# A passage from attention to a spectral layer: late output products grouped by half, one tile turned in the next PSUM pool, statistics taken later

## The chip, the core and the metric

The kernel runs on one core of one Trainium2 chip. The metric is the device time of one execution in microseconds (us), lower is better. Times of one kernel scatter: three runs of the kernel before gave 1471.8, 1475.76 and 1479.76 us, and the execution that was profiled took 1471.74 us.

## The reference

Four layers follow each other on `x` of 2048 rows by 576 columns, with a residual each: attention, spectral, attention, spectral.

```python
def _A_ref(x, wqkv, wo):              # H = 32 heads of 18, window W = 256
    q, k, v = (x @ wqkv) split into heads
    p = softmax(mask(q k^T * 18 ** -0.5))
    return (p v) @ wo
def _B_ref(x, w_r, w_i):
    X = rfft2(x) * (w_r + 1j * w_i)
    return irfft2(X, s=(S, D))
x = x + _A_ref(_layernorm(x), A_wqkv, A_wo)
x = x + _B_ref(_layernorm(x), B_w_r, B_w_i)
x = x + _A_ref(_layernorm(x), A_wqkv, A_wo)
x = x + _B_ref(_layernorm(x), B_w_r, B_w_i)
```

## The kernel before, in words

All orders are written out by hand: each engine runs its instructions in the order of the code, and semaphores that the framework adds from the tiles that are written and read make one engine wait for another. `layer_a` is an attention layer, `layer_b` the spectral layer that it calls at its end (`spectral`, line 1005). Both run twice, so that every passage from attention to the spectral layer occurs twice in the trace, near 477 to 500 us and near 1213 to 1237 us.

The passage is the output projection `o @ wo` plus residual, for 16 tiles of 128 rows. The class `Out` (line 442) holds it:

- `load` fetches a tile's attention output and its residual rows `x`; `tail` (GpSimd) and `turn` (TensorE transposes, then a copy and a subtraction) make the split stationary operands; `turn_last` and `split_last` do the same for the last 128 columns, which the last head group delivers at the very end. In the profile all stationary operands, weights and constants of this stage lie in one buffer `oroom`, everything in full precision (attention output, `x`, statistics) in `ofree`.
- A tile's projection is 28 products of 128x288: 14 pairs of a stationary and a moving operand, each for two halves of 288 columns. `early` (line 519) issues the 11 pairs that don't need the last columns, `late` (line 532) the other three pairs, then two adds on VectorE (line 538), one per half, of `x` and the half in PSUM, and the store. `steps` (line 513) is the loop over pairs and, inside, over the two halves.
- `unit` (line 555) does a whole tile: it takes one PSUM tile `ops`, 128 x 2 x 512, one half in each of two banks, calls `early` and `late`.
- `sums` and `stats` make the layer norm's statistics of the tile's new `x` (lines 545 and 546 on VectorE, a square root on ScalarE at line 547, two small VectorE operations at lines 551 and 552). `f0` (line 166) normalises and folds the row on ScalarE and GpSimd, and, for tile 0 only, with a subtraction on VectorE (line 173).

Tiles 0 to 2 are projected in the attention layer's PSUM pool, each half in a bank of its own tile (`ops0_0`, `ops0_1`, `ops1_S`, `ops1_E`, `ops2_E`, `ops2_pj`; lines 975 to 1004). The spectral layer then opens its own pool with the tags `mm` (three tiles of two banks), `tp` and `tq` (one bank each), and projects tiles 3 to 15 with `unit`, 13 a layer. Tiles 3 and 4 are interleaved with `norm` (that is `sums` and `f0`) of the first tiles (lines 241 to 255); from tile 5 on a loop over `t` (line 256) does, in this order: `unit(t + 4)`, `f1(t)` (transposes `tp`, `tq`), `sums`, `f3(t - 1)` (products `pz`), `f0(t + 4)`, `f2(t)` (products `pf`), and `ahead(t + 6)`, which loads, and turns the projection's operands of the tile two units ahead.

Where two banks of the old pool are taken over by a tile of the new one, that tile's first write waits until the old pool's readers are done.

Of the kernel before, what the change touches and what calls it, by code (L numbers as in the profile page):

```python
# [8 lines left out]
F32 = mybir.dt.float32  # L9
# [93 lines left out]
def layer_b(tc, src, dst, dcs, gc, ident, rh, rl, out, ic_d, fc_d, ga_d, m2_d, w_d, dram):  # L103

    nc = tc.nc
    V, A, T, P = nc.vector, nc.scalar, nc.tensor, nc.gpsimd
# [3 lines left out]
    with tc.tile_pool(name="bc", bufs=1) as cp, tc.tile_pool(name="bw", bufs=2) as wp, \  # L110
# [55 lines left out]
        def f0(n2, h):  # L166
            x, r, n = out.stats(n2)
            xn = wp.tile([128, D], F32, tag="ta", name=f"xn{n2}", bufs=3)
            A.activation(xn, x, AF.Identity, bias=n, scale=r)  # L169
            eo = h["eo"] = eos[n2 % 4]  # L170
            P.tensor_add(eo[:, 0, 1:288], xn[:, 1:288], xn[:, 575:288:-1])  # L171
            A.copy(eo[:, 0, 0:289:288], xn[:, 0:289:288])
            (P if n2 else V).tensor_sub(eo[:, 1, 0:287], xn[:, 1:288], xn[:, 575:288:-1])

            tl = h["tl"] = wp.tile([128, 2, 3, 33], F32, tag="td", name=f"tl{n2}", bufs=4)
            e = eo[:, :, 256:289]
            P.tensor_copy(tl[:, :, 0].bitcast(F32R), e)
            P.tensor_copy(tl[:, :, 2].bitcast(F32R), e)
            P.tensor_sub(tl[:, :, 1].bitcast(F32R), e, tl[:, :, 0])

        def turn(n2, x, tl):
            t4 = pp.tile([128, 512], F32, tag="tp", name=f"tp{n2}", bufs=1).rearrange("p (c a t) -> p c a t", c=2, a=2)
            tq = pp.tile([128, 512], F32, tag="tq", name=f"tq{n2}", bufs=1)[0:99, 0:256].rearrange("p (c t) -> p c t", c=2)
            for c in range(2):
                for a in range(2):
                    T.transpose(t4[:, c, a], x[:, c, 128 * a:128 * a + 128], ident)
            for c in range(2):
                T.transpose(tq[:, c], tl[:, c].rearrange("p a w -> p (a w)"), ident)
            et = wp.tile([128, 2, 4, 128], F32R, tag="tc", name=f"et{n2}", bufs=3)
            ett = wp.tile([99, 2, 128], F32R, tag="te", name=f"ett{n2}", bufs=3)  # L190
            A.copy(et[:, :, 0:2], t4)
            A.copy(ett, tq)
            V.tensor_sub(et[:, :, 2:4], t4, et[:, :, 0:2].bitcast(F32))
            return et, ett

        def rows(ps, ets, m):
            et, ett = ets
            for c in range(2):
                o = ps[:, c, 0:NF]
                seq = [(0, 0), (0, 2), (1, 1), (1, 3), (2, 0), (3, 1)]  # L200
                for q, (si, mi) in enumerate(seq):
                    T.matmul(o, et[:, c, si], m(5 * c + mi), start=q == 0, stop=False)  # L202
                T.matmul(o, ett[:, c], m(5 * c + 4)[0:99], start=False, stop=True)

        def f1(n2, h):
            eo, tl = h["eo"], h["tl"]
            h["et"] = turn(n2, eo, tl)

        def f2(n2, h):
            ps = pp.tile([128, 2, 512], F32, tag="mm", name=f"pf{n2}", bufs=3)  # L210
            rows(ps, h["et"], lambda k: dcs[k // 2][:, k % 2])
            h["yh"] = yh = wp.tile([128, 2, NF], F32R, tag="yh", name=f"yh{n2}", bufs=3)
            h["yl"] = yl = wp.tile([128, 2, NF], F32R, tag="yl", name=f"yl{n2}", bufs=3)
            A.copy(yh, ps[:, :, 0:NF])
            V.tensor_sub(yl, ps[:, :, 0:NF], yh.bitcast(F32))
# [21 lines left out]
        def norm(u):  # L237
            out.sums(u)
            f0(u, hs[u])

        f0(0, hs[0])
        out.load(5)
        norm(1)
        out.load(6)
        out.tail(5)
        out.unit(3, pp)
        norm(2)
        out.load(7)
        out.tail(6)
        f1(0, hs[0])  # L250
        out.unit(4, pp)
        f2(0, hs[0])
        out.ahead(5, pp)
        norm(3)
        out.tail(7)
        for t in range(1, NT - 4):
            u = t + 4
# [184 lines left out]
class Out:  # L442
# [67 lines left out]
        self.nc.scalar.copy(oL[:, 0:128], tp)  # L510
        self.nc.vector.tensor_sub(oL[:, 128:256], tp, oL[:, 0:128].bitcast(F32))

    def steps(self, u, ks, first, last):
        for i, (x, p, wk) in enumerate(ks):
            for n in range(2):
                self.nc.tensor.matmul(self.ps[u][n][:, 0:288], x, self.w[p][:, wk * D + n * 288:wk * D + n * 288 + 288],  # L516
                                      start=first and i == 0, stop=last and i == len(ks) - 1)

# [13 lines left out]
    def late(self, u):  # L532
        oL = self.oL[u % 3]
        h, l = oL[:, 0:128], oL[:, 128:256]
        self.steps(u, [(h, "h", 3), (l, "h", 3), (h, "l", 3)], False, True)
        x = self.x[u % 5]
        for n in range(2):
            self.nc.vector.tensor_add(x[:, n * 288:n * 288 + 288], x[:, n * 288:n * 288 + 288], self.ps[u][n][:, 0:288])
        self.nc.sync.dma_start(self.dstv[:, u], x)

# [29 lines left out]
def layer_a(tc, src, dst, wqk_d, wv_d, wo_d, dc_d, gc_d, dram, copy, wvs, wos, second, spectral):  # L570
    nc = tc.nc
    V, A, T, P = nc.vector, nc.scalar, nc.tensor, nc.gpsimd
# [7 lines left out]
    with ExitStack() as ctx:  # L580
# [129 lines left out]
        with ExitStack() as c2:  # L710
            wp = c2.enter_context(tc.tile_pool(name="a2", bufs=2))
            pp = c2.enter_context(tc.tile_pool(name="a2p", bufs=2, space=PSUM))
# [7 lines left out]
            for j in range(2):  # L720
                q = wp.tile([128, 2, S], F32R, name=f"qs{j}", bufs=1)
                k = wp.tile([128, 2, S], F32R, name=f"ks{j}", bufs=1)
# [171 lines left out]
            pj = [f for i in range(2, 9) for c in range(4) for f in proj(i, c, "E" if i == 2 and c % 2 else "pj", True)]  # L894
# [9 lines left out]
            out = Out(nc, ident, eps, bp, ov, o7v, srcv, dstv, wos, dc_d, gc_d)  # L904

            for t in range(-LEAD, NX + 2):
# [3 lines left out]
                n, c = divmod(t + 17, NT)  # L910
# [56 lines left out]
                if t - OB - 5 in (0, 1, 2):  # L967
                    u = t - OB - 5
# [8 lines left out]
            for k in range(4):  # L977
                tp = pp.tile([128, 512], F32, tag="E" if k in (1, 2) else "pj", name=f"tpz{k}", bufs=2)[0:32]
# [6 lines left out]
                             rc.to_broadcast([32, 4, 4, 18]))  # L985
            out.early(0, None, slice(4, 11))
            out.early(1, [pp.tile([128, 512], F32, tag=k, name=f"ops1_{k}", bufs=b) for k, b in (("S", 3), ("E", 2))])
            tp = pp.tile([128, 512], F32, tag="pj", name="tpl", bufs=2)
            for f in (out.turn_last, out.split_last):
                for u in range(3):  # L990
                    f(u, tp[:, 128 * u:128 * u + 128])
            out.early(2, [pp.tile([128, 512], F32, tag=k, name=f"ops2_{k}", bufs=2) for k in ("E", "pj")])
            out.turn(3, U, A)
            out.tail(4)
            for u in range(3):
                out.late(u)
                if u == 0:
                    out.turn_last(3, tp[:, 384:512])
                    out.split_last(3, tp[:, 384:512])
                    out.sums(u)  # L1000
                if u == 1:
                    out.turn_last(4, tp[:, 0:128])
                    out.split_last(4, tp[:, 0:128])
            out.turn(4, pp.tile([128, 512], F32, tag="E", name="tpa4", bufs=2), A)
        spectral(dst, out.dcs, out.gc, ident, out.rh, out.rl, out)
        ctx2.close()

# [1 line left out]
def prompt_kernel(tc, x, wqk, wv, wo, w, dc, ic, fc, gc, ga, m2, out):  # L1009
    with tc.tile_pool(name="dram", bufs=1, space=bass.MemoryType.DRAM) as dram, tc.manual_schedule():  # L1010
        t = [dram.tile([S, D], F32, name=f"x{i}") for i in range(3)]
        cr = {k: dram.tile(list(v.shape), F32R, name=k + "r") for k, v in (("dc", dc), ("ic", ic), ("gc", gc), ("ga", ga))}
        wvs, wos = [dram.tile([2, 128, 5 * D], F32R, name=k) for k in ("wvs", "wos")]
        for i, (s, a, d) in enumerate(((x, t[0], t[1]), (t[1], t[2], out))):
            with tc.tile_pool(name=f"dram{i}", bufs=1, space=bass.MemoryType.DRAM) as dr:
                layer_a(tc, s, a, wqk, wv, wo, cr["dc"], cr["gc"], dr, [(cr[k], v) for k, v in (("dc", dc), ("gc", gc), ("ic", ic), ("ga", ga))] if i == 0 else None, wvs, wos, i > 0,
                        lambda *args: layer_b(tc, args[0], d, *args[1:], cr["ic"], fc, cr["ga"], m2, w, dr))
# [18 lines left out]
```

## Time and profile before

| | us |
|---|---|
| three runs | 1471.8, 1475.76, 1479.76 (median 1475.76) |
| the profiled execution | 1471.74, of which the profile's span is 1470.0 |
| TensorE matmul busy | 1382.7 (94%) |
| VectorE, ScalarE, GpSimd busy | 950.0, 810.1, 714.0 |
| chain that ended last | PE 75%, DMA 9%, DVE 5%, ACT 4%, POOL 3% |

PE is TensorE's matmul, PEld its weight load, DVE VectorE, ACT ScalarE, POOL GpSimd, SP the engine that issues most DMAs. In a row of the timeline stand the start, the time until the end, the engine, the line, the operation, out<-in by the program's names (numbers left out), the shape, how many were merged into the row, and in brackets the idle time of the engine ahead of it with what ended it. A row with x and three numbers divided by strokes gives shortest, median and longest of a group in ns. The mean granted TensorE clock was 0.98 over the span.

### The profile page before, as it was taken

The numbers are of one execution on the slowest core, as the hardware profiler recorded it, in microseconds if no ns is written. First come the engines' busy times: TensorE is split into PE (matmuls) and PEld (weight loads), VectorE is DVE, ScalarE is ACT, GpSimd is POOL, SyncE is SP. The second block draws the span as 40 slices with busy tenths as digits, with TensorE's granted clock in tenths as the row PEclk, the third lists the DMA queues.
The fourth block names the chain that finished last, engine by engine and source line by source line (L and its number), as shares of the span: only waits on it lengthen the run. The fifth ranks groups of instructions, "written<-read, shape, count | busy, mean of one in ns | idle before, by whom it ended". The sixth has DMA issues, their size and how long they took to land.

```text
span 1470.0 us, 35320 instructions
## 1 busy us (share of the span) xinstructions
PE 1382.7 (94%) x12312; PEld 1066.8 (73%) x12312; DVE 950.0 (65%) x3105; ACT 810.1 (55%) x1895; POOL 714.0 (49%) x1205
## 2 busy tenths in 40 slices
PE   7999999999999899898789989999999998998988
PEld 7987666666655899648789866666666558997478
DVE  5348778788785566454543577777877864654545
ACT  5624677666678244225555237677666782442255
POOL 2356566566555333154611645665565562431546
PEclk9999999999999999998989999999999999999999
DMA  7866555555556366686574564555444564566865
GB/s 236 266 184 225 164 162 180 173 156 170 156 154 208 125 204 198 220 247 228 191 234 110 179 221 146 161 154 155 146 138 151 159 195 129 194 204 210 251 222 191
DMA packets 198644, 271.80 MB, mean 185 GB/s; under 512 B 86996, under 2 KB 109108, under 8 KB 197252
## 3 DMA queue, kind: packets, MB, share of 16 engines
q1 hardware_dynamic: 186236, 250.37, 54.7%
q10 hardware_dynamic: 11720, 15.95, 3.5%
q0 software_dynamic: 512, 3.23, 0.7%
q8 instruction: 99, 1.62, 0.5%
q14 instruction: 77, 0.63, 0.1%
HBM read 167.99 MB, written 103.86 MB: 185 GB/s over the span
## 4 chain that ended last, share of the span: by engine, by line
PE 75%; DMA 9%; DVE 5%; ACT 4%; POOL 3%; issue 2%; SPq 1%; ACTq 0%; DVEq 0%; POOLq 0%
PE pj L744 14%; PE U L860 11%; PE S L812 9%; PE E L840 9%; PE vps L700 8%; PE ops L516 6%; PE pf L202 3%; PE po L202 3%; PE pi L342 2%; PE tpo L870 2%; DMA qs<-mt 1%; ACT P L841 1%; PE pz L222 1%; DMA yd<-eo 1%; DVE ofree L297 1%
## 5 line engine op out<-in xcount | busy, mean ns | idle before, releaser
L814 DVE CUSTOM_DVE_ANT_0 jk<-S,mask 128x384 bf16<-128x384 f32 (+2 forms) x1024 | 497.7, 529 | 96.8 <-PE S L812 92.1
L841 ACT ACTIVATE P<-E 128x384 f32<-128x384 f32 (+2 forms) x1024 | 422.2, 476 | 174.5 <-PE E L840 143.2
L843 POOL TENSOR_SCALAR_AFFINE_SELECT P<-P 128x512 f32<-128x512 f32 x256 | 162.8, 636 | 276.1 <-ACT P L841 264.4
L812 PE MATMUL S<-ks,qs 63*128 63x384 f32 (+2 forms) x1024 | 238.0, 365 | 3.6 <-ACT P L841 0.8
L840 PE MATMUL E<-qs,ks 64*128 64x384 f32 (+2 forms) x1024 | 220.6, 395 | 7.7 <-DMA qs<-mt 5.1
L860 PE MATMUL U<-P,vq 128*19 128x128 f32 (+1 forms) x3840 | 204.0, 331 | 2.5 <-POOL P L846 2.0
L840 PEld LDWEIGHTS E<-qs,ks 64*128 64x128 f32 x1024 | 118.8, 184 | 84.4 <-issue 34.1
L812 PEld LDWEIGHTS S<-ks,qs 63*128 63x128 f32 x1024 | 132.2, 185 | 50.4 <-ACT P L841 22.9
L744 PE MATMUL pj<-xh,wqh 64*128 64x512 f32 (+1 forms) x640 | 165.1, 404 | 2.1 <-ACT vt L704 1.7
L860 PEld LDWEIGHTS U<-P,vq 128*19 128x19 f32 x3840 | 90.3, 98 | 96.1 <-issue 34.9
L846 POOL TENSOR_SCALAR_AFFINE_SELECT P<-P 128x512 f32<-128x512 f32 x224 | 142.5, 636 | 0.0
L744 PE MATMUL pj<-xl,wqh 64*128 64x512 f32 (+1 forms) x512 | 128.0, 394 | 0.0
L744 PE MATMUL pj<-xh,wql 64*128 64x512 f32 (+1 forms) x640 | 121.0, 392 | 0.0
L516 PE MATMUL ops<-oroom 128*128 128x288 f32 x784 | 115.3, 304 | 4.4 <-DVE oroom L499 3.0
L516 PEld LDWEIGHTS ops<-oroom 128*128 128x128 f32 x784 | 108.1, 194 | 6.2 <-DVE oroom L499 4.0
L744 PEld LDWEIGHTS pj<-xh,wqh 64*128 64x128 f32 (+1 forms) x640 | 87.3, 188 | 7.5 <-ACT vt L704 2.1
L171 POOL TENSOR_TENSOR eo<-xn 128x287 f32<-128x287 f32 x32 | 26.2, 817 | 132.3 <-ACT xn L169 127.4
L814 DVE DVE_READ_ACCUMULATOR2_ANT m<- 128x1 f32 x1024 | 85.1, 83 | 0.0
L744 PEld LDWEIGHTS pj<-xh,wql 64*128 64x128 f32 (+1 forms) x640 | 73.1, 186 | 7.4
L758 POOL TENSOR_TENSOR sg<-sg 128x512 fp32r<-128x512 f32 x56 | 72.2, 1289 | 4.7
L744 PEld LDWEIGHTS pj<-xl,wqh 64*128 64x128 f32 (+1 forms) x512 | 71.0, 188 | 3.8
L700 PE MATMUL vps<-wvh,xh 128*128 128x288 f32 x320 | 72.7, 309 | 0.0
(176 smaller groups left out, 2467.7 us busy)
## 6 DMA issues: line engine op xcount, KB each, us to landing
qk_d<-sg SPq DMA_DIRECT2D x56, 512.0 KB
qs<-qk_d SPq DMA_DIRECT2D x384, 72.0 KB
ks<-qk_d SPq DMA_DIRECT2D x384, 72.0 KB
v_d<-vt SPq DMA_DIRECT2D x32, 304.0 KB
vq<-v_d SPq DMA_DIRECT2D x16, 608.0 KB
yd<-ye SPq DMA_DIRECT2D x32, 290.0 KB
wt<-in_w SPq DMA_DIRECT2D x16, 580.0 KB
x<-ofree SPq DMA_DIRECT2D x32, 288.0 KB
```

The costliest lines, as they stand in the source:

```text
L202: T.matmul(o, et[:, c, si], m(5 * c + mi), start=q == 0, stop=False)
L516: self.nc.tensor.matmul(self.ps[u][n][:, 0:288], x, self.w[p][:, wk * D + n * 288:wk * D + n * 288 + 288], start=first and i == 0, stop=la ...
L700: T.matmul(ps[:, n, 0:288], xT(xk, c), w[:, wk, n * 288:(n + 1) * 288], start=i == 0, stop=i == len(ks) - 1)
L744: T.matmul(ps, w[r, wk], xT(xk, cs)[r], start=s == 0, stop=s == len(ks) - 1)
L758: (P if halves else V).tensor_sub(sg[:, 1], su, sg[:, 0].bitcast(F32))
L812: T.matmul(ps[:, 0:N], q[b:b + 63, pair, i * 128:i * 128 + 128], k[b:b + 63, pair, lo:hi], start=True, stop=True)
L814: V.tensor_tensor_reduce(out=jk[:, 0:N], in0=ps[:, 0:N], in1=mask[:, 384 - N:384], scale=1.0, scalar=-3e38, op0=ALU.add, op1=ALU.max, accu ...
L840: T.matmul(ps[:, 0:nq], k[b:b + 64, pair, j * 128:j * 128 + 128], q[b:b + 64, pair, j * 128:j * 128 + nq], start=True, stop=True)
L841: A.activation(p[:, hl_, 0:nq], ps[:, 0:nq], AF.Exp, scale=SC)
L843: P.affine_select(out=p[:, :, 0:128], in_=p[:, :, 0:128], pattern=[[0, 4], [1, 128]], compare_op=ALU.is_ge, fill=0.0, base=0, channel_mult ...
L846: P.affine_select(out=p[:, :, 256:384], in_=p[:, :, 256:384], pattern=[[0, 4], [-1, 128]], compare_op=ALU.is_gt, fill=0.0, base=0, channel ...
L860: T.matmul(U[32 * h:32 * h + 19, (q0 % 4) * 128:(q0 % 4) * 128 + 128 * (q1 - q0)], vts[n][:, j, h], pt[n, j][:, h, (q0 - j) * 128:(q1 - j) ...
```

## The change

It touches both passages and every `unit`. In five parts:

1. `late` no longer issues its six products pair by pair with the halves alternating, but the three products of half 0, the add of half 0, then the three products of half 1 and the add of half 1. `steps` gets an argument `halves` for it. This holds for tiles 0 to 2 and for all 13 tiles that `unit` projects.
2. The first six pairs of tile 2's early products go ahead of the turn of the last columns of tiles 0 to 2, the other five stay behind it; tile 2 therefore takes its PSUM buffers before `tpl` does.
3. The late products of tiles 0 to 2 follow each other; the last columns' turn and split of tile 4 and the turn of tile 4, which stood between and behind them, move to the start of the spectral layer as `out.ahead(4, pp)`, into the new pool's `tp` and `tq`. These are now the new pool's first tiles: `tp` and `tq` get banks 0 and 1, and `mm` banks 2 to 7 (before: `mm` 0 to 5, `tp` 6, `tq` 7).
4. The statistics of tile 0 come behind all late products and adds of tiles 0 to 2; `unit(3)` comes behind `norm(2)`, that is behind the statistics of tiles 1 and 2, instead of ahead of it.
5. `ahead(5)` comes ahead of `f2(0)` instead of behind it.

```diff
+        out.ahead(4, pp)
         out.load(5)
         norm(1)
         out.load(6)
         out.tail(5)
-        out.unit(3, pp)
         norm(2)
         out.load(7)
         out.tail(6)
+        out.unit(3, pp)
         f1(0, hs[0])
         out.unit(4, pp)
+        out.ahead(5, pp)
         f2(0, hs[0])
-        out.ahead(5, pp)
...
-    def steps(self, u, ks, first, last):
+    def steps(self, u, ks, first, last, halves=(0, 1)):
         for i, (x, p, wk) in enumerate(ks):
-            for n in range(2):
+            for n in halves:
...
-        self.steps(u, [(h, "h", 3), (l, "h", 3), (h, "l", 3)], False, True)
         x = self.x[u % 5]
         for n in range(2):
+            self.steps(u, [(h, "h", 3), (l, "h", 3), (h, "l", 3)], False, True, (n,))
             self.nc.vector.tensor_add(x[:, n * 288:n * 288 + 288], x[:, n * 288:n * 288 + 288], self.ps[u][n][:, 0:288])
...
+            out.early(2, [pp.tile([128, 512], F32, tag=k, name=f"ops2_{k}", bufs=2) for k in ("E", "pj")], slice(0, 6))
             tp = pp.tile([128, 512], F32, tag="pj", name="tpl", bufs=2)
             for f in (out.turn_last, out.split_last):
                 for u in range(3):
                     f(u, tp[:, 128 * u:128 * u + 128])
-            out.early(2, [pp.tile([128, 512], F32, tag=k, name=f"ops2_{k}", bufs=2) for k in ("E", "pj")])
+            out.early(2, None, slice(6, 11))
...
                     out.split_last(3, tp[:, 384:512])
-                    out.sums(u)
-                if u == 1:
-                    out.turn_last(4, tp[:, 0:128])
-                    out.split_last(4, tp[:, 0:128])
-            out.turn(4, pp.tile([128, 512], F32, tag="E", name="tpa4", bufs=2), A)
+            out.sums(0)
```

The lines below are the program as built, engine by engine. First, TensorE around tile 8's unit in the loop, before. `tqo9` is the turn of the next tile, `ops8` the 28 products of the unit, `tp4` and `tq4` the transposes of `f1(4)`, `pz3` the products of `f3(3)`; what is in brackets is the semaphore that a row waits for.

```order
L496 MATMUL tqo9_8981<-ident_77,ofree_7363 128x128 [waits PE_49]
L516 MATMUL ops8_8991<-oroom_7362 128x288 x28
L186 MATMUL tp4_9023<-ident_77,eo0_8466 128x128 [waits DVE_49]
L186 MATMUL tp4_9023<-ident_77,eo0_8466 128x128 x3
L188 MATMUL tq4_9024<-ident_77,tl4_8705 99x128 [waits DVE_49]
```

The same place in the changed kernel:

```order
L497 MATMUL tqo9_8982<-ident_77,ofree_7363 128x128 [waits PE_49]
L517 MATMUL ops8_8992<-oroom_7362 128x288 x25
L517 MATMUL ops8_8992<-oroom_7362 128x288 [waits DVE_49]
L517 MATMUL ops8_8992<-oroom_7362 128x288 x2
L186 MATMUL tp4_9024<-ident_77,eo0_8456 128x128 [waits Activation_49]
```

The 28 products stood in one run without a wait; now the 26th, the first late product of half 1, carries a wait for VectorE. The count that it waits for is the one that the add of half 0 of the same tile raises; the same wait stands in each of the 26 units.

Second, VectorE where the spectral layer begins, before. `tpl` and `tpa4` are turned operands that are split, the adds read `ops0` to `ops2`, lines 545 and 546 are statistics.

```order
L538 TENSOR_TENSOR ofree_7363<-ofree_7363,ops0_1_8286 128x288
L511 TENSOR_TENSOR oroom_7362<-tpl_8365,oroom_7362 128x128
L545 BN_STATS ofree_7363<-ofree_7363 128x6 x2
L546 BN_AGGR ofree_7363<-ofree_7363 128x2
L538 TENSOR_TENSOR ofree_7363<-ofree_7363,ops1_S_8341 128x288
L538 TENSOR_TENSOR ofree_7363<-ofree_7363,ops1_E_8342 128x288
L511 TENSOR_TENSOR oroom_7362<-tpl_8365,oroom_7362 128x128
L538 TENSOR_TENSOR ofree_7363<-ofree_7363,ops2_E_8375 128x288
L538 TENSOR_TENSOR ofree_7363<-ofree_7363,ops2_pj_8376 128x288
L499 TENSOR_TENSOR oroom_7362<-tpa4_8444,oroom_7362 128x384
```

And in the changed kernel, the end of this stretch: the statistics of tile 2, the adds of tile 3, and the split for `f1(0)`.

```order
L546 BN_STATS ofree_7363<-ofree_7363 128x6 x2
L547 BN_AGGR ofree_7363<-ofree_7363 128x2
L552 RECIPROCAL ofree_7363<-ofree_7363 128x1
L553 SCALAR_TENSOR_TENSOR ofree_7363<-ofree_7363 128x1
L539 TENSOR_TENSOR ofree_7363<-ofree_7363,ops3_8526 128x288 x2
L193 TENSOR_TENSOR et0_8566<-tp0_8558,et0_8566 128x2x256
```

Further ahead VectorE now runs the six adds of tiles 0 to 2 without statistics between them, then the statistics of tile 0 and its subtraction (line 173), the split of tile 4, and the same four rows for tile 1. Both adds of tile 3 stand behind all of this; before, they stood ahead of the statistics of tile 2.

Third, TensorE at the change of pools in the changed kernel: the late products of tile 2, the turn of tile 4 (`tpo4`, `tqo4`) and unit 3.

```order
L517 MATMUL ops2_E_8365<-oroom_7362 128x288 [waits Activation_49]
L517 MATMUL ops2_E_8365<-oroom_7362 128x288 x2
L517 MATMUL ops2_pj_8366<-oroom_7362 128x288 x3
L494 MATMUL tpo4_8475<-ident_77,ofree_7363 128x128 [waits DMAHW1_49,DVE_49,Activation_49]
L494 MATMUL tpo4_8475<-ident_77,ofree_7363 128x128 x2
L495 MATMUL tpo4_8475<-ident_77,ofree_7363 128x128 [waits Pool_49]
L497 MATMUL tqo4_8476<-ident_77,ofree_7363 128x128
L517 MATMUL ops3_8526<-oroom_7362 128x288 x25
L517 MATMUL ops3_8526<-oroom_7362 128x288 [waits DVE_49]
L517 MATMUL ops3_8526<-oroom_7362 128x288 x2
```

The turn of tile 4 has moved from the end of the old pool to the start of the new one, and its wait for VectorE is for the last add of tile 2; unit 3 follows it at once, with the wait ahead of its 26th product.

## The prediction

> **What bounds the kernel now.** I read the page first, then the windows and the timeline of the loop that projects tiles 5 to 15, then the timeline of the passage on TensorE, VectorE and ScalarE. The page's first part and the last item's row of its chain of waits:
>
> ```profile
> PE 1382.7 (94%) x12312; PEld 1066.8 (73%) x12312; DVE 950.0 (65%) x3105; ACT 810.1 (55%) x1895; POOL 714.0 (49%) x1205
> PE 75%; DMA 9%; DVE 5%; ACT 4%; POOL 3%; issue 2%; SPq 1%; ACTq 0%; DVEq 0%; POOLq 0%
> ```
>
> TensorE is the bound on the whole; what a wait on it costs is decided stage by stage. One period of the loop, as a row of the windows (columns: busy time of PE, PEld, DVE, ACT, POOL, then clock and DMA), and the unit inside it on TensorE and on VectorE:
>
> ```profile
> 540.00:547.73 7.73, 7.73 (x61) 7.66 (x60) 4.74 (x13) 3.42 (x8) 2.83 (x7) 1.00 0.70 221
> 542.26 3.96 PE L516 MATMUL ops<-oroom 128*128 128x288 f32 x28
> 546.05 0.60 PE L186 MATMUL tp<-ident,eo 128*128 128x128 f32 x4
> 545.04 0.28 DVE L511 TENSOR_TENSOR oroom<-tqo,oroom 128x128 fp32r<-128x128 f32 x1
> 546.25 0.82 DVE L538 TENSOR_TENSOR ofree<-ofree,ops 128x288 f32<-128x288 f32 x2 [0.93 <-PE ops L516]
> ```
>
> TensorE is busy for 7.73 of 7.73 us and has no wait in the loop; the 28 products run through, the transposes follow at once, and the adds run beside them on a VectorE that was idle for 0.93 us. So anything that holds TensorE inside a unit lengthens the loop by its full size. In the passage it is the other way round: TensorE stands idle and VectorE and ScalarE set the pace.
>
> **Part one of the change: halves in `late`.** No instruction is added; but the first late product of half 1 now waits for the add of half 0 of the same tile, 13 times a layer. Behind it on TensorE are queued the rest of the unit and the loop's transposes and products; for them, VectorE and ScalarE wait. The trace of before has no such wait, but all its pieces: the product's and the add's duration, the start after a wait (the three products of the row at 1245.35), and the lag from VectorE to TensorE (517.33 and 0.56 make 517.89, the turn starts at 517.94).
>
> ```profile
> L516 PE MATMUL ops<-oroom x784: 288/295/442, 476.5 to 1329.1; 128*128 128x288 f32 x196
> L538 DVE TENSOR_TENSOR ofree<-ofree,ops x56: 442/448/455, 489.8 to 1329.8; 128x288 f32<-128x288 f32 x56
> 1245.35 0.66 PE L516 MATMUL ops<-oroom 128*128 128x288 f32 x3 [0.24 <-DVE oroom L499]
> 517.33 0.56 DVE L499 TENSOR_TENSOR oroom<-tpo,oroom 128x384 fp32r<-128x384 f32 x1 [1.02 <-ACT oroom L498]
> 517.94 0.55 PE L493 MATMUL tpo<-ident,ofree 128*128 128x128 f32 x3 [1.32 <-DVE oroom L499]
> ```
>
> Counted from the start of half 0's last product: its end 0.295; the add starts 0.03 later (the 28 products end at 546.22, the add starts at 546.25) and takes 0.448; TensorE starts 0.05 after it. In a running row the next product would have started after (3.96 - 0.295) / 27 = 0.136. After a wait three products take 0.66, in a running row 0.295 + 2 x 0.136 = 0.57: 0.09 more. Sum: 0.295 + 0.03 + 0.448 + 0.05 - 0.136 + 0.09 = 0.78 us for each unit. Bounds: 0.45, the add alone, if the rest were covered, and 1.8, if the add stands in VectorE's queue behind a split that itself waits 1.02 for ScalarE, as at 517.33. In the loop VectorE is free (its last operation ends at 545.32, the add is wanted at about 545.8), so I take 0.78. Units 4 to 15: 12 x 0.78 = 9.4 us a layer. Unit 3 belongs to the passage.
>
> **Parts two to four: the passage.** Layer one before, on TensorE from tile 1's last early product to tile 0's transposes:
>
> ```profile
> 484.04 0.29 PE L516 MATMUL ops_E<-oroom 128*128 128x288 f32 x1
> 484.76 0.55 PE L505 MATMUL tpl<-ident,ofree 128*128 128x128 f32 x3 [0.43 <-DMA ofree<-o_d]
> 488.06 0.49 PE L493 MATMUL U<-ident,ofree 128*128 128x128 f32 x3
> 490.86 0.33 PE L505 MATMUL tpl<-ident,ofree 128*128 128x128 f32 x1 [0.50 <-DVE oroom L511]
> 492.52 0.55 PE L493 MATMUL tpa<-ident,ofree 128*128 128x128 f32 x3 [0.53 <-DVE ofree L538]
> 494.44 5.50 PE L516 MATMUL ops<-oroom 128*128 128x288 f32 x28 [1.27 <-DVE oroom L499]
> 499.78 0.60 PE L186 MATMUL tp<-ident,eo 128*128 128x128 f32 x4
> ```
>
> The removed waits: 0.43 (the last columns' DMA; twelve products, 12 x 0.136 = 1.6 us, now cover it), 0.50 and 0.53 (tile 4's last columns and turn), 1.27 (unit 3 behind the turn's split). These are 2.7 us, and in layer two 3.8, since the DMA came later there:
>
> ```profile
> 1219.94 0.29 PE L516 MATMUL ops_E<-oroom 128*128 128x288 f32 x1
> 1221.68 0.52 PE L505 MATMUL tpl<-ident,ofree 128*128 128x128 f32 x3 [1.45 <-DMA ofree<-o_d]
> 1236.65 0.60 PE L186 MATMUL tp<-ident,eo 128*128 128x128 f32 x4
> ```
>
> What is late next is VectorE's queue. The durations for it, on VectorE and on ScalarE:
>
> ```profile
> 489.32 0.56 DVE L499 TENSOR_TENSOR oroom<-U,oroom 128x384 fp32r<-128x384 f32 x1 [2.14 <-ACT oroom L498]
> 489.79 0.81 DVE L538 TENSOR_TENSOR ofree<-ofree,ops 128x288 f32<-128x288 f32 x2
> 490.52 0.28 DVE L511 TENSOR_TENSOR oroom<-tpl,oroom 128x128 fp32r<-128x128 f32 x1
> 490.72 0.81 DVE L545 BATCH_NORM_STATS2 ofree<-ofree 128x6 f32<-128x288 f32 x2
> 491.56 0.21 DVE L546 BATCH_NORM_AGGREGATE ofree<-ofree 128x2 f32<-128x12 f32 x1
> 495.68 0.46 DVE L173 TENSOR_TENSOR eo<-xn 128x287 f32<-128x287 f32 x1 [0.98 <-ACT xn L169]
> 497.48 0.16 DVE L551 RECIPROCAL ofree<-ofree 128x1 f32<-128x1 f32 x1 [0.36 <-ACT ofree L547]
> 497.67 0.16 DVE L552 SCALAR_TENSOR_TENSOR ofree<-ofree 128x1 f32<-128x1 f32 x1
> 493.21 0.59 ACT L498 CAST oroom<-tpa 128x512 fp32r<-128x512 f32 x1 [0.96 <-PE tpa L494]
> 494.78 0.87 ACT L169 ACTIVATE xn<-ofree 128x576 f32<-128x576 f32 x1 [0.98 <-DVE ofree L552]
> ```
>
> TensorE in the changed kernel: twelve products from 484.18, three turns, ten products and tile 3's turn bring it to 488.0 (488.5 before); the 18 late products and one turn run through, the last one starts near 490.5. Tile 3's subtraction starts near 488.85 (after the turn, ScalarE's 0.59 and two lags), then come six adds 0.37 apart and one split, 0.20: the last add ends near 491.8. Tile 4's turn, first in the new pool, waits for it: 1.2 us. After 0.55 for the turn unit 3 starts at 492.4, and its 25th product at 495.8.
>
> Its 26th waits for an add that is queued behind everything in VectorE's new order: tile 0's statistics (0.84 + 0.21), the square root's round trip 0.36, two small operations 0.35, then ScalarE's 0.87 and VectorE's 0.46 on tile 0, near 494.9; ScalarE's copy of tile 4's turn, which stands behind the 0.87, and the two splits, near 495.85; tile 1's statistics with their round trip, 0.84 + 0.21 + 0.36 + 0.35 = 1.76, and tile 2's, another 1.7; then the add, 0.45, near 499.7. So TensorE waits about 4.0 us at unit 3 and reaches tile 0's transposes near 500.25, against 499.78 before: 0.45 us later. In layer two the chain has the same length from the same start (1219.94 is 735.90 after 484.04), and before lay at 1236.65, which is 0.97 more: 0.5 us earlier. Together 0 us; bounds 1.5 us each way a passage, by what of VectorE's queue I counted double or not at all.
>
> The clock, before (third column from the right), in the passage and at a stretch of the loop with waits:
>
> ```profile
> 490.00:495.00 5.00, 2.71 (x18) 2.00 (x17) 4.19 (x18) 1.25 (x4) 0.00 (x0) 1.00 0.47 175
> 495.00:500.00 5.00, 5.00 (x28) 5.00 (x28) 1.74 (x7) 2.20 (x5) 2.94 (x6) 0.66 0.61 167
> 495.50:498.00 2.50, 2.50 (x12) 2.50 (x12) 1.72 (x6) 0.77 (x4) 1.76 (x4) 0.50 0.66 199
> 1250.00:1255.00 5.00, 3.31 (x24) 2.84 (x24) 3.39 (x10) 2.41 (x7) 2.47 (x7) 1.00 0.26 99
> ```
>
> TensorE was busy for 2.71 of 5 us, and then the clock was half for about 3.4 us (a mean of 0.66 over 5 us); 28 products took 5.50 instead of 3.96 us: 1.5 us, paid once a passage and contained in the 499.78. In the changed kernel a single wait of 4.0 us stands there. A slow stretch that begins in it falls partly on the wait itself and only partly on unit 4. Between 0 and 1.5 us a passage I take 0.5 for the rest that falls on products: 1.0 for both. The Trainium skill, "TensorE: Matmul & The Clock Gate", section "Part 1: The HAM clock gate", says that an idle window of about 3.4 us halves the clock and a busy one restores it, and that the windows run freely; the 3.4 us here agree. By that rule the wait would cost one such window, and a second one if the first holds too little work: up to 1.5 us a passage.
>
> **Part five.** `ahead(5)` ahead of `f2(0)` puts 14 products between tile 5's turn and unit 5, which waited twice there:
>
> ```profile
> 507.73 0.53 PE L516 MATMUL ops<-oroom 128*128 128x288 f32 x2 [0.67 <-ACT oroom L498]
> 508.51 3.65 PE L516 MATMUL ops<-oroom 128*128 128x288 f32 x26 [0.24 <-DVE oroom L499]
> ```
>
> Both go, with their two late starts: 0.67 + 0.24 + 2 x 0.09 = 1.1 us a layer. The cover is `f2(0)`, 14 x 0.136 = 1.9 us; without it the 1.1 us would come back.
>
> **The sum.** A layer: +9.4 - 1.1 = +8.3, twice 16.6; passages 0; clock +1.0. Together +17.6 us. On the profiled execution, 1471.74, that makes 1489.3; the median of the runs shown lies 4.0 us above it, and I forecast on it: 1475.76 + 17.6 = 1493.4, rounded 1493 us.
>
> **Rivals.**
>
> 1. *The halves overlap.* If the 26th product did not have to wait for the add, everything else of the change would stay: unit 3 would run through from 492.4, tile 0's transposes would follow near 496.2, that is 3.6 us earlier in layer one and 4.5 in layer two, and 1.1 a layer from part five: -10.3 us, 1465.5. For it: the two halves lie in two banks, and the add of half 0 would really be out of the way while half 1 is multiplied. The Trainium skill, "Perfetto Trace Analysis", section "Matmuls", asks for just this: independent groups should rotate through PSUM banks so that the evacuation of one overlaps the next group's matmuls; by that rule the time is this rival's. Against it: the built program has the wait on the 26th product of each unit. It decides if that semaphore is already raised when the product's turn comes, and the add can't start before the 25th product ends, 0.16 us after the 26th is due. Chance 0.04.
> 2. *The wait is made good.* TensorE's rows in the loop touch without being at their peak, so the loop might be held by something else that leaves 0.78 us: then only the passages remain, 1475.8 to 1477. Against it: no other engine is busy for more than 4.74 of 7.73 us, and the products' spacing of 0.136 is regular. Chance 0.04.
> 3. *The low clock stays.* If the waits keep TensorE at half speed for a second window in each passage, another 2 x 1.5 us: 1496.4. In the loop the wait is 0.7 of 8.5 us, and with TensorE busy for 3.31 of 5 us, from 1250 on, the clock stayed at 1.00, so I don't expect it there. Chance 0.12.
>
> **How the numbers follow.** The forecast has 0.80, rival three 0.12, one and two 0.04 each. From 1486 (the lowest run, 1471.8, plus 16.6 less 2 for the passages) to 1499 (the highest run, 1479.76, plus 17.6 and 1.5). A difference of 0.5%, 7.4 us, is about what a measurement of this kernel tells from none. Slower by more: forecast and rival three, 0.92; within: rival two, 0.04; faster by more: rival one, 0.04.
>
> **What would show it.** Right: a wait of about 0.7 us on line 517 in each unit with VectorE's line 539 as its releaser, a loop period of 8.5 us, about 4 us of the same wait at unit 3, no wait for the DMA at `tpl`. Wrong: a period of 7.7 us, or tile 0's transposes before 498 us.

## The result and the profile after

The changed kernel takes 1495.5 us (median of 4 runs, 1493.44 to 1499.76), the kernel before 1475.0 (4 runs, 1471.8 to 1479.76): a ratio of 1.0131, 95% interval 1.011 to 1.0151, so slower by 20.5 us. The profiled execution took 1494.23 us with a span of 1492.5 us.

The first row of the page of the changed kernel, each engine's busy time:

```profile
PE 1389.1 (93%) x12312; PEld 1072.9 (72%) x12312; DVE 953.1 (64%) x3105; ACT 809.8 (54%) x1895; POOL 712.7 (48%) x1205
```

The same 12312 products, 22.5 us more span, and only 6.4 us more busy time on TensorE: most of the loss is idle time of the bound engine. Where it waits, the list of waits says (who waited, for whom, us in total, times, longest):

```profile
PEld ops L517 <- DVE ofree L539: 28.6, 26, 4.1
PE ops L517 <- DVE ofree L539: 22.5, 26, 3.9
```

Neither row exists before. They are the 26 units: 2 x 3.9 us at unit 3, and 14.7 us in the other 24. One period of the loop as a row of the windows, columns as before:

```profile
535.30:543.83 8.53, 7.98 (x60) 7.68 (x60) 4.81 (x12) 3.41 (x8) 2.82 (x7) 1.00 0.59 197
```

The next unit of the changed kernel in the timeline of TensorE:

```profile
548.27 3.56 PE L517 MATMUL ops<-oroom 128*128 128x288 f32 x25
552.37 0.66 PE L517 MATMUL ops<-oroom 128*128 128x288 f32 x3 [0.55 <-DVE ofree L539]
```

And the add of its half 0 in the timeline of VectorE, with the split ahead of it:

```profile
551.04 0.28 DVE L512 TENSOR_TENSOR oroom<-tqo,oroom 128x128 fp32r<-128x128 f32 x1
551.86 0.46 DVE L539 TENSOR_TENSOR ofree<-ofree,ops 128x288 f32<-128x288 f32 x1 [0.54 <-PE ops L517]
```

The 25 products end at 551.83, the add runs from 551.86 to 552.32, the 26th product starts at 552.37. VectorE had been idle for 0.54 us before that add: the add is not late, TensorE stands still for its whole length. The period is 8.53 us instead of 7.73, 0.80 a unit.

The passage of layer one in the timeline of TensorE (stretches between the rows are left out):

```profile
487.27 0.49 PE L506 MATMUL tpl<-ident,ofree 128*128 128x128 f32 x3
...
493.21 0.52 PE L494 MATMUL tpo<-ident,ofree 128*128 128x128 f32 x3 [1.19 <-issue]
...
493.70 3.55 PE L517 MATMUL ops<-oroom 128*128 128x288 f32 x25
501.15 0.83 PE L517 MATMUL ops<-oroom 128*128 128x288 f32 x3 [3.90 <-DVE ofree L539]
501.78 1.05 PE L186 MATMUL tp<-ident,eo 128*128 128x128 f32 x4
...
502.92 4.44 PE L517 MATMUL ops<-oroom 128*128 128x288 f32 x25
...
510.85 3.49 PE L517 MATMUL ops<-oroom 128*128 128x288 f32 x25
```

And what VectorE does ahead of the add that unit 3 waits for:

```profile
492.67 0.44 DVE L539 TENSOR_TENSOR ofree<-ofree,ops_pj 128x288 f32<-128x288 f32 x1
493.03 0.81 DVE L546 BATCH_NORM_STATS2 ofree<-ofree 128x6 f32<-128x288 f32 x2
...
497.18 0.81 DVE L546 BATCH_NORM_STATS2 ofree<-ofree 128x6 f32<-128x288 f32 x2
...
498.87 0.81 DVE L546 BATCH_NORM_STATS2 ofree<-ofree 128x6 f32<-128x288 f32 x2
...
500.50 0.23 DVE L553 SCALAR_TENSOR_TENSOR ofree<-ofree 128x1 f32<-128x1 f32 x1
500.66 0.44 DVE L539 TENSOR_TENSOR ofree<-ofree,ops 128x288 f32<-128x288 f32 x1
```

The wait for the DMA at `tpl` is gone, the turn of tile 4 waits 1.19 us, the 26th product of unit 3 waits 3.90 us for an add that stands behind the statistics of three tiles; unit 5's products (510.85) run without the two waits of before. The rows 501.78 and 502.92 show a half clock, the second in its first 2 us: four transposes in 1.05 us instead of 0.60, 25 products in 4.44 instead of 3.56.

To tell the touched part from the rest, I use the stretch from the first `ops` product to the start of the last `pz` product, read from the groups of the timeline (first and last start). Of the kernel before, layer one and layer two:

```profile
L516 PE MATMUL ops<-oroom x392: 288/294/442, 476.5 to 591.7; 128*128 128x288 f32 x196
L222 PE MATMUL pz<-yh,oroom x64: 292/299/398, 512.6 to 613.8; 128*128 128x290 f32 x64
L516 PE MATMUL ops<-oroom x392: 288/295/442, 1212.4 to 1329.1; 128*128 128x288 f32 x196
L222 PE MATMUL pz<-yh,oroom x64: 291/299/397, 1249.5 to 1351.2; 128*128 128x290 f32 x64
```

Of the changed kernel, the same:

```profile
L517 PE MATMUL ops<-oroom x392: 288/295/589, 478.0 to 603.4; 128*128 128x288 f32 x196
L222 PE MATMUL pz<-yh,oroom x64: 291/298/402, 516.0 to 626.6; 128*128 128x290 f32 x64
L517 PE MATMUL ops<-oroom x392: 288/295/610, 1219.8 to 1346.5; 128*128 128x288 f32 x196
L222 PE MATMUL pz<-yh,oroom x64: 291/298/398, 1259.1 to 1368.7; 128*128 128x290 f32 x64
```

613.8 - 476.5 = 137.3 and 138.8 before, 148.6 and 148.9 after: +11.3 and +10.1, together +21.4 of the 22.5 us. The remaining 1.1 is a balance of stages that the change does not touch.

Two executions of the runs below took more than twice as long as the others (3293.97 us of the kernel before, 3095.96 us of the one with unit 3 earlier); no median or ratio in this document counts them.

### The profile page after: what moved, and what is told of

Same layout as the page of the kernel before. It is cut to its first block, busy times and chain, and to the rows that moved or that the text cites. A ratio compares the mean times of both kernels' runs of the same rounds, so it can differ in the third digit from the quotient of the medians.

```text
span 1492.5 us, 35316 instructions
## 1 busy us (share of the span) xinstructions
PE 1389.1 (93%) x12312; PEld 1072.9 (72%) x12312; DVE 953.1 (64%) x3105; ACT 809.8 (54%) x1895; POOL 712.7 (48%) x1205
## 4 chain that ended last, share of the span: by engine, by line
PE 76%; DMA 8%; DVE 6%; ACT 4%; POOL 2%; issue 2%; SPq 1%; ACTq 0%; DVEq 0%; POOLq 0%
PE pj L745 14%; PE U L861 11%; PE E L841 9%; PE S L813 9%; PE vps L701 8%; PE ops L517 7%; PE pf L202 3%; PE po L202 3%; PE tpo L871 2%; PE pi L343 2%; ACT P L842 1%; DMA oroom<-wos 1%; DMA yd<-ze 1%; PE pz L222 1%; DMA ofree<-yd 1%
## 5 line engine op out<-in xcount | busy, mean ns | idle before, releaser
L842 ACT ACTIVATE P<-E 128x384 f32<-128x384 f32 (+2 forms) x1024 | 422.2, 477 | 169.1 <-PE E L841 137.3
L517 PE MATMUL ops<-oroom 128*128 128x288 f32 x784 | 121.5, 307 | 22.5 <-DVE ofree L539 22.5
L171 POOL TENSOR_TENSOR eo<-xn 128x287 f32<-128x287 f32 x32 | 26.1, 815 | 154.4 <-ACT xn L169 137.5
```

What stands on the lines that cost most here:

```text
L842: A.activation(p[:, hl_, 0:nq], ps[:, 0:nq], AF.Exp, scale=SC)
```

## The experiments

Theory W is the prediction's: TensorE waits inside each unit for the add of half 0, and at unit 3 for VectorE's queue. The rivals: the loss sits in the passages and their clock (P), or order by half is slow in itself (O). The stretch of each layer, in us, and the times (each ratio is against runs of the kernel before on the same chip, whose medians were 1475.9 us for the first four experiments and 1474.0 us for the last four):

| kernel | stretch, layer one | layer two | sum | time, median | ratio to before, 95% interval |
|---|---|---|---|---|---|
| before | 137.3 | 138.8 | 276.1 | 1475.0 | |
| changed | 148.6 | 148.9 | 297.5 | 1495.5 | 1.0131 (1.011 to 1.0151) |
| units by pair | 134.4 | 134.5 | 268.9 | 1469.3 | 0.9949 (0.993 to 0.9968) |
| halves only | 146.8 | 149.0 | 295.8 | 1499.6 | 1.0151 (1.0129 to 1.0173) |
| two tiles | 137.5 | 135.5 | 273.0 | 1471.1 | 0.9975 (0.9956 to 0.9994) |
| unit 3 earlier | 145.8 | 145.8 | 291.6 | 1494.8 | 1.0121 (1.0094 to 1.0147) |
| filled wait | 147.1 | 146.2 | 293.3 | 1490.5 | 1.0108 (1.0086 to 1.0131) |
| part five alone | 138.3 | 135.9 | 274.2 | 1473.2 | 0.9983 (0.9967 to 1.0) |
| by pair, reordered | 133.9 | 134.0 | 267.9 | 1467.8 | 0.9952 (0.9935 to 0.997) |
| covered halves | 139.5 | 140.0 | 279.5 | 1480.9 | 1.0043 (1.0028 to 1.0059) |

A stretch also holds what the clock did in it. Some 3.4 us at half clock, called a low window here, cost about 1.5 us in a passage (the kernel before has one in each: 28 products in 5.50 and 5.48 us instead of 3.96). A low window behind the last unit costs about 1.2: from the last `ops` product to the last `pz` product it is 23.2 to 23.4 us with one and 22.1 or 22.2 without (21.3 in covered halves, which has none). Such a late window lies in layer one of the changed kernel, units by pair, two tiles, unit 3 earlier, filled wait, part five alone and by pair, reordered, and in layer two of units by pair, halves only and by pair, reordered. So differences of one or two us between rows can be the clock's.

### Units by pair

```diff
     def late(self, u):
...
+        ks = [(h, "h", 3), (l, "h", 3), (h, "l", 3)]
+        if u > 2:
+            self.steps(u, ks, False, True)
         for n in range(2):
-            self.steps(u, [(h, "h", 3), (l, "h", 3), (h, "l", 3)], False, True, (n,))
+            if u < 3:
+                self.steps(u, ks, False, True, (n,))
```

> The changed kernel, but in the 13 tiles that unit projects the six late products alternate between the halves again and both adds follow them; tiles 0 to 2 and everything else stay as changed. Theory W (the wait for the add of half 0 costs the time): no wait on VectorE's add inside a unit; period of the loop 7.73 us instead of 8.53; 24 units at 0.80 us make -19.2, and the 3.9 us wait at unit 3 goes twice, -7 to -8: 1467 to 1470 us, so some 0.5% faster than the kernel before. Theory P (the passage with its later statistics and the clock costs the time, the waits in the units are covered otherwise): the period falls, but the time stays at 1485 or above.

Measured: 1469.3 us. One period of the loop as a row of the windows:

```profile
546.75:554.47 7.72, 7.72 (x62) 7.64 (x61) 4.73 (x12) 3.41 (x8) 2.82 (x7) 1.00 0.68 221
```

The passage in the timeline of TensorE:

```profile
497.01 3.96 PE L517 MATMUL ops<-oroom 128*128 128x288 f32 x28
500.81 0.60 PE L186 MATMUL tp<-ident,eo 128*128 128x128 f32 x4
...
506.46 0.55 PE L494 MATMUL tpo<-ident,ofree 128*128 128x128 f32 x3 [1.12 <-DVE et L193]
```

The period is that of before, the 3.9 us wait is gone, and the rest of the change, kept whole, makes the kernel faster than before. Theory P falls: with no product waiting inside a unit, the later statistics cost little. What they do cost is the last row's wait at the turn of tile 5, 1.12 us.

### Halves only

The kernel before, with nothing but part one's edit of `steps` (as in the change, left out here) and `late`:

```diff
...
-        self.steps(u, [(h, "h", 3), (l, "h", 3), (h, "l", 3)], False, True)
         x = self.x[u % 5]
         for n in range(2):
+            self.steps(u, [(h, "h", 3), (l, "h", 3), (h, "l", 3)], False, True, (n,))
```

> The kernel before with part one of the change alone: the late products grouped by half for all tiles, nothing else moved. Theory W: 13 waits of 0.55 us a layer (0.8 us with what belongs to them), 26 x 0.78 = 20.3: 1495 to 1497 us, period 8.53 us, and nothing above 1 us at unit 3, whose adds are not queued behind statistics there. Theory P: the passages are those of before, so the time is 1475 to 1482.

Measured: 1499.6 us, +22.3 by the ratio (19.0 to 25.5), stretch +19.7. One period, as a row of the windows:

```profile
546.18:554.70 8.52, 7.98 (x59) 7.67 (x59) 4.82 (x12) 3.41 (x8) 2.80 (x7) 1.00 0.67 207
```

Unit 3 and unit 4 in the timeline of TensorE:

```profile
503.23 0.66 PE L516 MATMUL ops<-oroom 128*128 128x288 f32 x3 [0.55 <-DVE ofree L538]
...
508.83 0.66 PE L516 MATMUL ops<-oroom 128*128 128x288 f32 x3 [0.96 <-DVE ofree L538]
```

Part one alone makes the whole loss, as W has it; its size agrees with the 20.3 us expected. The kernel before has a low window in each passage, this one has only one behind layer two's last unit, and without these the stretch grows by about 21.5 us (19.7 + 3.0 - 1.2). The median itself is 2.6 us above the upper end I gave, which the interval allows.

### Two tiles

```diff
     def unit(self, u, pp):
-        ps = pp.tile([128, 2, 512], F32, tag="mm", name=f"ops{u}", bufs=3)
-        self.early(u, [ps[:, 0], ps[:, 1]])
+        ps = [pp.tile([128, 2, 512], F32, tag="mm", name=f"ops{u}_{n}", bufs=3)[:, 0] for n in range(2)]
+        self.early(u, ps)
         self.late(u)
```

> The changed kernel with its order by half, but a unit's two halves go into two PSUM tiles of the same pool (one bank of each is used) instead of the two banks of one tile. Theory W, in the form that the wait belongs to the tile and not to the order or the banks: the 26th product no longer waits, the add of half 0 runs beside the products of half 1, period 7.73 us, 1466 to 1470 us, as with the order by pair. Rival O (order by half, or an add that reads PSUM beside products, is slow in itself): the period stays above 8.2 us and the time at 1485 or above.

Measured: 1471.1 us. A period of the loop, as a row of the windows:

```profile
540.00:547.73 7.73, 7.73 (x61) 7.66 (x60) 4.76 (x12) 3.42 (x9) 2.82 (x7) 1.00 0.74 220
```

A unit's products and adds in the timeline:

```profile
547.02 3.96 PE L517 MATMUL ops<-oroom 128*128 128x288 f32 x28
550.62 0.85 DVE L539 TENSOR_TENSOR ofree<-ofree,ops 128x288 f32<-128x288 f32 x2 [0.53 <-PE ops L517]
```

The start of unit 4 in the passage of layer one, on TensorE:

```profile
502.50 0.38 PE L517 MATMUL ops<-oroom 128*128 128x288 f32 x1
505.59 5.14 PE L517 MATMUL ops<-oroom 128*128 128x288 f32 x27 [2.71 <-DVE ofree L539]
```

The order of products and adds is the changed kernel's, each half has a bank of its own as there, and the wait is gone: the add of half 0 starts at 550.62, while the products of half 1 run until 550.98. So rival O falls, and the wait belongs to the PSUM tile as the unit of the semaphores. The time is 1.1 us above the upper end expected, and the stretch 4.1 us above that of units by pair. The rows show a new wait: a unit now takes two of three buffers, so unit 4's second product writes into unit 3's first buffer and waits 2.71 us for the add behind VectorE's queue (2.70 in layer two). In layer one a low window follows it: 27 products in 5.14 us, in layer two 3.84. And the overlap bought nothing: the loop has the same 7.73 us as by pair.

### Unit 3 earlier

```diff
+        out.unit(3, pp)
         norm(2)
         out.load(7)
         out.tail(6)
-        out.unit(3, pp)
```

> The changed kernel with unit(3) ahead of norm(2), where it stood before; its two adds then stand ahead of tile 2's statistics on VectorE. Theory W: the wait at unit 3 shrinks from 3.9 us by the statistics of tile 2 with their round trip, 1.7 us, to about 2.2, in both passages; tile 0's transposes 1.7 us earlier; the loop is as in the changed kernel: -3.4 us, 1492. If the half clock behind that wait comes only from a wait near 4 us, its 1.5 us a passage go too: 1489. Theory P, that statistics ahead of unit 3 make most of the loss: 1485 or below.

Measured: 1494.8 us. Unit 3 in layer one and in layer two, and there also the first 25 products of unit 4:

```profile
504.43 0.66 PE L517 MATMUL ops<-oroom 128*128 128x288 f32 x3 [2.12 <-DVE ofree L539]
...
1249.52 0.66 PE L517 MATMUL ops<-oroom 128*128 128x288 f32 x3 [2.12 <-DVE ofree L539]
...
1250.60 5.08 PE L517 MATMUL ops<-oroom 128*128 128x288 f32 x25
```

The wait is 2.12 us where 2.2 were expected, and the stretch falls by 2.8 and 3.1 us, 5.9 together. VectorE's queue is thus what sized the 3.9 us. The wait accounts for 1.78 us a layer, 3.6 of the 5.9; most of the rest is the clock, which stayed at 1.00 in layer one's passage. In layer two it was half for about 3.4 us (the row at 1250.60: 5.08 us instead of 3.56), so a half clock there needs no wait near 4 us, and the further 3 us that the expectation named were not gained in full. The time does not show it, and the 1492 us expected were missed by 2.8: in the profiled execution the attention of layer one, which is the same in both kernels, ended 5.0 us later than in the changed kernel's (first `ops` product at 483.0 instead of 478.0), and the interval of the ratio overlaps the changed kernel's.

### Filled wait

26 products without use, in a tile that nobody reads, between the early and the late products of unit 3:

```diff
         self.early(u, [ps[:, 0], ps[:, 1]])
+        if u == 3:
+            d = pp.tile([128, 2, 512], F32, tag="mm", name="fill", bufs=3)
+            for i in range(26):
+                self.nc.tensor.matmul(d[:, i % 2, 0:288], self.oT[0][:, 0:128], self.w["h"][:, 0:288], start=True, stop=True)
         self.late(u)
```

> The changed kernel with 26 idle products of 128x288 more between the 25th and the 26th product of unit 3, into a PSUM tile that nobody reads: 26 x 0.136 = 3.5 us of the 3.9 us wait are filled with work that adds nothing to the result. Theory C (half speed follows idle TensorE): no half clock between unit 3 and tile 1's transposes in either passage, where the changed kernel lost 1.6 and 2.7 us; the wait at unit 3 shrinks to about 0.5 us with unchanged end; the stretch from the first ops product to the last pz product 147 us or less per layer instead of 148.6 and 148.9; the whole 1492. Rival: the half clock comes at that place however busy TensorE is: the same low stretch, and the time unchanged.

Measured: 1490.5 us, 147.1 and 146.2 us of stretch. The passage on TensorE:

```profile
495.41 3.59 PE L562 MATMUL fill<-oroom 128*128 128x288 f32 x26
...
499.94 0.66 PE L517 MATMUL ops<-oroom 128*128 128x288 f32 x3 [0.55 <-DVE ofree L539]
500.44 0.60 PE L186 MATMUL tp<-ident,eo 128*128 128x128 f32 x4
...
501.01 3.56 PE L517 MATMUL ops<-oroom 128*128 128x288 f32 x25
```

From 478 to 600 us, and in layer two's passage, no microsecond has a granted clock under 1.00 (layer one's stretch holds a low window later, from 608.1 to 611.6), and the transposes of tile 0 come 23.7 us after the first product, as in the changed kernel (23.8): 3.5 us of idle products cost nothing, since they lay in the wait. This fits theory C, but doesn't prove it: the kernels with the units by pair also have no half clock in their passages, with waits of 1.2 us.

### Part five alone

The kernel before with one line moved:

```diff
+        out.ahead(5, pp)
         f2(0, hs[0])
-        out.ahead(5, pp)
```

> The kernel before with part five alone: ahead(5) ahead of f2(0). As predicted: the waits of 0.67 and 0.24 us at unit 5 go, 1.1 us a layer earlier, 1473 on a kernel of 1475 to 1476, less than the times can tell; read in the timeline as 11.1 us instead of 12.2 from tile 0's to tile 1's transposes. Rival: the turn of tile 5 now stands ahead of f2(0) and waits there for VectorE's split of tile 0 (L193), since both use the buffer tp; then part of the 1.1 comes back as a wait at tpo, as the 1.12 us in the kernel with the units by pair suggest: 11.8 us, 0.4 a layer.

Measured: 1473.2 us, not to be told from before. Its timeline on TensorE:

```profile
504.44 0.60 PE L186 MATMUL tp<-ident,eo 128*128 128x128 f32 x4
...
509.54 0.55 PE L493 MATMUL tpo<-ident,ofree 128*128 128x128 f32 x3 [0.58 <-DVE et L193]
...
515.74 0.60 PE L186 MATMUL tp<-ident,eo 128*128 128x128 f32 x4
```

From transposes to transposes 11.30 us instead of 12.22, and 11.48 instead of 12.25 in layer two (1236.69 to 1248.17): 0.92 and 0.77 gained, between the two expectations. The moved turn does wait for the split of tile 0, 0.58 and 0.76 us; without that, the move would be worth 1.5.

### By pair, reordered

The units by pair, and besides:

```diff
+        out.unit(3, pp)
+        f1(0, hs[0])
         norm(2)
         out.load(7)
         out.tail(6)
-        out.unit(3, pp)
-        f1(0, hs[0])
         out.unit(4, pp)
```

> The units by pair as in the first experiment, and besides unit(3) and f1(0) ahead of norm(2). In that experiment the turn of tile 5 waits 1.12 us for the split of tile 0's transposes, which stands behind tile 2's statistics (1.7 us) on VectorE. With tile 2's statistics behind it this wait should go: -1.1 us a layer, 1467 where the first experiment gives 1469. If VectorE's queue is not what holds the split, the wait stays and so does the time.

Measured: 1467.8 us, stretches 133.9 and 134.0. The turn of tile 5:

```profile
505.17 0.49 PE L494 MATMUL tpo<-ident,ofree 128*128 128x128 f32 x3
...
506.19 0.33 PE L495 MATMUL tpo<-ident,ofree 128*128 128x128 f32 x1 [0.53 <-POOL ofree L430]
```

The wait of 1.12 us for VectorE is gone, half of it comes back as one of 0.53 for GpSimd's part of the turn, and 0.5 us a layer is left. It is faster than both kernels, by 7 us against before (ratio 0.9952, 0.9935 to 0.997); against the first experiment, which the times can't tell from it, only the stretch is shorter.

### Covered halves

The order by half as changed, but with the loop's transposes between the halves:

```diff
-            out.unit(u, pp)
-            f1(t, hs[t])
+            out.unit(u, pp, lambda: f1(t, hs[t]))
...
-    def late(self, u):
+    def late(self, u, mid=None):
...
             self.nc.vector.tensor_add(x[:, n * 288:n * 288 + 288], x[:, n * 288:n * 288 + 288], self.ps[u][n][:, 0:288])
+            if n == 0 and mid:
+                mid()
...
```

> The changed kernel with its order by half; in the loop, for tiles 5 to 15, the transposes of f1(t) now stand between the late products of half 0 and those of half 1, instead of behind both. Theory W (the price is TensorE standing idle while VectorE adds): six transposes, 0.57 us from the first of them to the next product, cover the wait of 0.55, period 7.75 to 7.9 us, 22 x 0.7 = 15 us less: 1480. Rival (each add of half 0 costs its 0.8 us wherever it stands): period 8.53, 1495.

Measured: 1480.9 us. One unit in the loop on TensorE, and the start of the next:

```profile
541.19 3.56 PE L516 MATMUL ops<-oroom 128*128 128x288 f32 x25
544.59 0.60 PE L186 MATMUL tp<-ident,eo 128*128 128x128 f32 x4
...
545.30 0.66 PE L516 MATMUL ops<-oroom 128*128 128x288 f32 x3
...
548.95 3.56 PE L516 MATMUL ops<-oroom 128*128 128x288 f32 x25
```

Six transposes stand where TensorE stood idle, and the period is 7.76 us instead of 8.53, so 22 units give back 0.77 each, 16.9 us of the 18.0 by which the stretch falls (297.5 - 279.5). In the loop the add of half 0 itself costs next to nothing (0.03 us a period above the 7.73 of before); standing still for it does.

## Why the prediction was right, point by point

- **The direction and its cause.** Right, and shown by taking it away in three ways (by pair, two tiles, covered) and by adding it alone (halves only). The 1493 forecast stands against 1495.5 measured.
- **0.78 us a unit.** Measured 0.80 in the nine units 7 to 15 (8.53 - 7.73). The steps are all there: 0.03 from product to add, 0.46 the add, 0.05 back, idle 0.55, and the slower start of three products (0.66).
- **12 units alike.** Not quite. Unit 6 waits 1.35 us, since VectorE's add stands behind a split there that had itself come late, behind an operation (line 215) that waited 1.75 us for ScalarE; an add behind a late split was the case of the prediction's upper bound, but it expected none in the loop. It made 0.3 us more in layer one and nothing in layer two, where a wait of 0.67 that stood behind that unit before went.
- **The passage.** 4.0 us of wait at unit 3 were predicted, 3.90 measured; 1.2 at the turn of tile 4, measured 1.19. Tile 0's transposes come 23.8 us after the first `ops` product instead of 23.3: +0.5, predicted +0.45. In layer two 24.3 instead of 24.3, predicted -0.5; 0.4 of the difference is the three products of unit 3, which took 1.09 us at a low clock instead of 0.66.
- **The clock: the term that was mis-sized.** +0.5 a passage was taken, because a slow stretch would fall partly on the wait. It began near the wait's end (at 501.5, the wait ended at 501.15; at 1242.2, the wait ended at 1243.23) and fell on work. Unit 3's last products and unit 4's first 25 in layer two, from the timeline of TensorE:

```profile
1243.23 1.09 PE L517 MATMUL ops<-oroom 128*128 128x288 f32 x3 [3.90 <-DVE ofree L539]
...
1245.25 5.24 PE L517 MATMUL ops<-oroom 128*128 128x288 f32 x25
```

The transposes of tile 0, up to unit 4's first product, took 1.14 and 1.13 us instead of 0.57, unit 4's 25 products 4.44 and 5.24 instead of 3.56: 1.45 us in layer one and 2.24 in layer two, 3.7 instead of 1.0. Layer two's low stretch ran until 1249.0, twice as long as the 3.4 us of before: rival three, in one of the two passages.
- **Part five, -1.1 a layer.** From tile 0's to tile 1's transposes lie unit 4 and unit 5: 12.22 us became 13.61, in layer two 12.25 became 14.38. Less the clock (1.45, 2.24) and two units at 0.80 this leaves -1.7 for part five. The prediction added up the two waits and their late starts only. Counted from start to start, the rows of before lose 1.4 us there: from 506.79 to 508.51 TensorE starts one transpose and two products, which take 0.3 us in a running row. The work ahead of a wait runs to its end first, which the sum for a unit counted and this one did not. And the products of `f2(0)`, now behind the turn, took 1.98 us instead of 2.19. The moved turn could have waited for tile 0's split, as it did when the line moved alone, but in the changed kernel its row (508.41) has no such wait, probably because the wait inside unit 4 gave the split time; that is argued, not shown.
- **The sum.** Predicted +17.6, in the stretches +21.4: clock 2.7 more, 1.1 for another low window (611 to 614 us) behind layer one's last unit, passages 0.6, units and part five together about -0.6 off. Each alone is less than the runs scatter. That the medians differ by 20.5 us and the profiled spans by 22.5 is within that scatter as well, and errors of both signs partly cancelled: a part of the closeness to +17.6 is luck.
- **The rivals.** Rival one, that the halves overlap, does not hold for this kernel, but holds as soon as each half has a tile: the stretch is then 3.1 us shorter than before instead of 21.4 longer. It is not the 10.3 us of this rival's price, in part since unit 4's new wait takes 2.7 us in each layer. The sentence of the Trainium skill ("Perfetto Trace Analysis", section "Matmuls") on groups that rotate through PSUM banks agrees with that run, where each half has a tile and a bank of its own; two halves in the two banks of one tile did not overlap in any of the 26 units of the changed kernel. Rival two, that the wait is made good, fell with the period of 8.53 us; its own time, 1475.8 to 1477, left out the 2.2 us that part five was to save in the passages.

## What to carry to other kernels

Before splitting work by halves so that an evacuation can start earlier, look at what the semaphores count: if both halves lie in one tile, the second half waits for the read of the first, and an order that alternates hides what the new one exposes. On an engine that is busy for all of a loop's period, an earlier start of the other engine is worth nothing (here 7.73 us a period by pair and by half in two tiles), and each idle moment inside the loop is worth its full length; work that is due anyway, put into the gap, takes the price away. A product that waits for an engine with a long queue costs that queue, so put what it waits for ahead of the work that nobody needs yet.

## What the runs showed of the hardware that was not expected

Half clock on TensorE came in stretches of about 3.4 us or twice that, and whether one came in a passage differed between runs of the same passage: the kernel before had one in each layer (495.1 to 498.5 and 1232.4 to 1235.8), halves only none, part five alone one of twice the length (6.68 us for 28 products) in layer one and none in layer two. In the four passages that held the 3.9 us wait unfilled (changed kernel, covered halves) it came each time, in the other sixteen five times; that is a hint that the long wait brings it, and no proof. TensorE need not stand idle throughout for it: in the 3.4 us ahead of the low stretch it had been busy for 1.6 and 1.7 us in the kernel before and 1.9 in layer one of part five alone, against 0.2 to 0.6 in the four passages with the 3.9 us wait.

The first `ops` product, ahead of which the kernels hardly differ, started between 476.5 and 483.0 us in the ten profiles. A difference of a few us in the time of one run says nothing here; the stretch around the change, read from the trace, told apart what the medians could not, as far as the low windows in it are counted too.
